# Windowed attention with two MLP layers on one core: the weight clamps of the first layer on GpSimd, and nine tiles' masks as a bf16 product

## The chip, the core and the metric

The kernel runs on one core of one Trainium2 chip. The metric is the device time of one execution in microseconds. TensorE is PE in the profile, VectorE DVE, ScalarE ACT, GpSimd POOL and SyncE SP; SP issues every load and store of this kernel.

## The reference, cut to what matters

Attention in a window of 32 keys to either side, with 32 global positions for each batch, then two MLP layers. B, H, Sl, Sg, D = 4, 8, 512, 32, 64.

```python
s_ll = scale * np.matmul(q_l, k_l.transpose(0, 1, 3, 2))
pos = np.arange(Sl)
mask = np.abs(pos[:, None] - pos[None, :]) <= window
s_ll = np.where(mask, s_ll, -1000000000.0)
s_lg = scale * np.matmul(q_l, k_g.transpose(0, 1, 3, 2))
a_l = sm(np.concatenate([s_lg, s_ll], axis=-1))
out_l = np.matmul(a_l, np.concatenate([v_g, v_l], axis=2))
...
h = x @ w_in                       # 512 -> 1024
solu = h * softmax(h)
ln = (solu - mu) / np.sqrt(var + 1e-06) * g_ln
x = ln @ w_out                     # 1024 -> 512
...
h = x @ w_in                       # 512 -> 2048
g = np.where(h >= 1, h, np.where(h <= -1, 0.0, (h + 1) ** 2 / 4))
out = g @ w_out                    # 2048 -> 512
```

All inputs are float32, the weights come as float64 words in pairs of 32-bit integers.

## The kernel before, in words

There are 16 tiles of 128 local positions and one more tile with the global positions of all four batches. The work goes through three stages that overlap.

**Attention**, tile by tile (`attention`, called with a tile and a part). `scores(t)` makes the scores of eight heads in a PSUM tile S (128 x 1024, two banks, from the ring psH of two, which the first MLP layer's h uses too): 32 small fp32 products, in which each block of 32 queries meets 128 keys. The outer blocks of 32 of these 128 keys need the window's triangles; the addition at L298 on VectorE puts them in. Then VectorE takes the maximum (nm), ScalarE the exponentials with their sum (e, rs). `gscores` makes the scores G of the global queries, `ptrans` transposes e (pPT), `pv` makes the output o and xn, `xtrans` transposes it into xy (pxT).

**The first MLP layer**, tile by tile in periods p: `b1` makes h with 24 products of 128x512 and the softmax and normalisation behind it, with a small power on GpSimd (rstd, L436) in the middle; `b3` transposes (plnT) and splits; `b4` makes yT for two tiles at a time. Products are made with split fp32r values: `split` writes a high part on ScalarE and the rest on GpSimd or VectorE (L137), and `mm3` adds three products.

**The second MLP layer** walks over 16 steps for each of three blocks of tiles (`h2`, `accum`), from 324 us on.

**Weights** come in pieces of 128x512. `fetch` issues a load of the double words into a staging buffer (raw), `convert` makes float32 of it: Abs on ScalarE (L147), a clamp of the exponent's range (L151), a shift (L155) and two combinations with the words (L157, L159), all four on VectorE, then for w_out of the first layer a scale on GpSimd (L163), then `split`. The first 16 pieces are those of the first MLP layer: eight of w_in in the lead, eight of w_out in the periods p = 0 to 3. The staging ring has three buffers, and SyncE's queue waits for L159, which frees one.

**What sets the order.** TensorE and SyncE run in the order in which the program is written, by small strings of letters: `START`, `LEAD_ORDER` for the first four tiles' attention (which also converts eight pieces), `ORDER_0` for p < 3 and `ORDER_1` behind. In period p, `attention` works on tile p + 4 and calls `scores(t + 2)`. On VectorE, ScalarE and GpSimd a scheduler orders the instructions; `behind` keeps a conversion behind an earlier VectorE instruction where `vec.gate` is set. `keep_warm` puts products of zeros (bf16, 128x512) ahead of the scores of the first five tiles.

The masks are built at the start on GpSimd, with 24 affine selects.

Of the kernel before, what the change touches and what calls it, by code (L numbers as in the profile page):

```python
# [8 lines left out]
F32 = mybir.dt.float32  # L9
# [51 lines left out]

STASH = range(5, 11)

WARM_S = [12, 4, 3, 4, 3]
WARM_P = [2, 5]

# [5 lines left out]
def kernel(ctx, tc, qk, vwin, qkg, vloc, vglo, w1i, w1o, g_ln, w2i, w2o, out):  # L72
# [13 lines left out]
    dram = ctx.enter_context(tc.tile_pool(name="dram", bufs=1, space=bass.MemoryType.DRAM))  # L86

    ident = const.tile([P, P], F32, name="ident")
    masks = const.tile([P, 3, 2, 32], F32, name="masks")
    nhalf = const.tile([P, 1], F32, name="nhalf")  # L90
    warm = const.tile([P, 1], F32, name="warm")
    gsb = const.tile([P, K1], F32, name="gsb")
# [10 lines left out]
    for c in range(4):  # L103
        for m in range(3):
            blk = masks[32 * c:32 * c + 32, m]
            nc.gpsimd.affine_select(out=blk[:, 0], in_=blk[:, 0], pattern=[[1, 32]], compare_op=ALU.is_ge, fill=NEG, base=0, channel_multiplier=-1)
            nc.gpsimd.affine_select(out=blk[:, 1], in_=blk[:, 1], pattern=[[-1, 32]], compare_op=ALU.is_ge, fill=NEG, base=0, channel_multiplier=1)
    nc.gpsimd.memset(masks[0:32, 1, 0], NEG)
    nc.gpsimd.memset(masks[96:128, 2, 1], NEG)

    class Ordered:

# [23 lines left out]
        act(out=hi, in_=src, func=AF.Copy)  # L136
        eng.tensor_tensor(out=lo, in0=src, in1=hi.bitcast(F32), op=ALU.subtract)  # L137

    def convert(weights, eng=nc.gpsimd):

        ws = []
        for (hi, lo), raw, scale in weights:
            t = stg.tile([P, 512], I32, tag="w32", name="w32")
            words = raw.rearrange("p (n two) -> p n two", two=2)
            ws.append((hi, lo, words[:, :, 0], words[:, :, 1], t, t.bitcast(F32), scale))
        for hi, lo, low, high, t, tf, scale in ws:
            first = nc.scalar.activation(out=tf, in_=high.bitcast(F32), func=AF.Abs)  # L147
            if vec.gate == "both" and vec.act is not None:
                behind(first, vec.act)
        for hi, lo, low, high, t, tf, scale in ws:  # L150
            first = nc.vector.tensor_scalar(tf, tf, WORD_LO, WORD_HI, ALU.max, ALU.min)  # L151
            if vec.gate and vec.last is not None:
                behind(first, vec.last)
        for hi, lo, low, high, t, tf, scale in ws:
            nc.vector.tensor_scalar(t, t, 3, 0x3FFFFFF8, ALU.logical_shift_left, ALU.bitwise_and)  # L155
        for hi, lo, low, high, t, tf, scale in ws:
            nc.vector.scalar_tensor_tensor(out=t, in0=high, scalar=-0x40000000, in1=t, op0=ALU.bitwise_and, op1=ALU.bitwise_or)  # L157
        for hi, lo, low, high, t, tf, scale in ws:
            nc.vector.scalar_tensor_tensor(out=t, in0=low, scalar=29, in1=t, op0=ALU.logical_shift_right, op1=ALU.bitwise_or)  # L159
        for hi, lo, low, high, t, tf, scale in ws:  # L160
            t3 = tf.rearrange("p (k n) -> p k n", k=hi.shape[1])
            if scale is not None:
                nc.gpsimd.tensor_tensor(out=t3, in0=t3, in1=scale.unsqueeze(2).to_broadcast(list(t3.shape)), op=ALU.mult)  # L163
            split(hi, lo, t3, eng)
# [11 lines left out]
            fetched.append((make, raw, scale))  # L176
        del todo[:n]

    def weights(n=1, eng=nc.gpsimd):
        while n > 0:  # L180
            m = min(n, 2)
            fetch(max(0, m - len(fetched)))
            convert([(make(), raw, scale) for make, raw, scale in fetched[:m]], eng)
            del fetched[:m]
            n -= m

# [94 lines left out]
    def scores(t):  # L281
        g = SEQ[t] % NB
        qT = qkT[t][:, :HP * P].rearrange("p (h c n) -> p h c n", h=HP, c=4)
        kT = key_blocks(t)
        S = psH.tile([P, 2, HP, P], F32, tag="H", name="S")
        if t < len(WARM_S):
            keep_warm(S[:, 0].rearrange("p h n -> p (h n)"), WARM_S[t])
        for hp in range(HP):
            for par in range(2):
                r = slice(64 * par, 64 * par + 64)  # L290
                for ci in range(4):
                    w = WSTART[ci]
                    mm(out=S[32 * ci:32 * ci + 32, par, hp], lhsT=qT[r, hp, ci],
                       rhs=kT[r, hp, w:w + 4].rearrange("p c d -> p (c d)"), start=True, stop=True)
        Sh = S.rearrange("p a h n -> p (a h) n")
        m = masks[:, 1 if g == 0 else 2 if g == NB - 1 else 0]
        edge = Sh.rearrange("p h (c d) -> p h c d", d=32)[:, :, 0:4:3]
        tt(out=edge, in0=edge, in1=m.unsqueeze(1).to_broadcast([P, H, 2, 32]), op=ALU.add)  # L298
        e = eT[t] = m1.tile([P, H, P], F32, tag="e", name="e", bufs=3)
        rs[t] = sm.tile([P, H], F32, tag="rs", name="rs")  # L300
        nm = sm.tile([P, H], F32, tag="nm", name="nm")
        vec.tensor_reduce(nm, Sh, AX.X, ALU.max, negate=True)
        vec.tensor_scalar(nm, nm, SCALE, None, ALU.mult)
        for h in range(H):
            act(out=e[:, h], in_=Sh[:, h], func=AF.Exp, bias=nm[:, h:h + 1], scale=SCALE, accum_out=rs[t][:, h:h + 1])
        vec.tensor_scalar(rs[t], rs[t], EPS_SM, None, ALU.add)
        vec.reciprocal(rs[t], rs[t])
# [276 lines left out]
    with tc.manual_schedule(engines={mybir.EngineType.PE, mybir.EngineType.SP}):  # L584
# [39 lines left out]
        for t in range(LEAD):  # L624
            n = CONV[t]
            for i, c in enumerate(LEAD_ORDER):
                if c in "012":
                    attention(t, int(c))
                elif c == "g":
                    attention(t, 4)  # L630
                elif c == "3" and t > 0:
                    attention(t - 1, 3)
                elif c == "w":
                    m = -(-n // LEAD_ORDER[i:].count("w"))
                    n -= m
                    weights(m)
                    fetch(3 + len(rooms) - len(fetched))


# [1 line left out]
        for p in range(NT):  # L641
# [3 lines left out]
            for i, c in enumerate(order):  # L645
# [18 lines left out]
                elif c == "4" and p >= 3:  # L664
                    b4(*divmod(p - 3, 2))
                elif c == "5" and p > 0:
                    b3(p - 1)
                elif c == "w":
                    if t == NL:
                        xtrans(NL)  # L670
                        at.close()
                        tc.swap_default_side()
                        w2ap = ExitStack()
                        w2a = w2ap.enter_context(tc.tile_pool(name="w2a", bufs=1, reuse_waits="tile"))
                        tc.swap_default_side()
                        weights2(15, in_pool(w2a))
                    m = -(-n // order[i:].count("w"))
                    n -= m
                    if todo or fetched:
                        weights(m)  # L680
                        fetch(3 + len(rooms) - len(fetched))
                    elif waiting or stashed or converted:
                        stash()
# [119 lines left out]
```

## Time and profile before

| | |
|---|---|
| runs | 718.05, 718.90 and 719.64 us, median 718.90 |
| the profiled execution | 718.96 us, its span 716.8 us |
| mean granted clock of TensorE | 0.983 |
| TensorE busy | 687.2 us, 96% of the span |
| weight loads of TensorE | 604.7 us, 84% |
| VectorE | 410.5 us, 57% |
| ScalarE | 311.3 us, 43% |
| GpSimd | 180.9 us, 25% |
| DMA | 72.54 MB, 101 GB/s over the span |

The span runs from the first to the last instruction; 2.2 us of the execution lie around it. A busy share is an average over stages with different limits, and is to be read by stretch.

### The profile page before, as it was taken

Reading aid. Unit: us, or ns where it says so; the run is one execution under the profiler, and the core shown is the slowest. Engines: PE = TensorE matmul, PEld = TensorE weight load, DVE = VectorE, ACT = ScalarE, POOL = GpSimd, SP = SyncE. Lnnn points to the kernel's source line nnn. Section 1 sums busy time; section 2 is a strip of 40 time slices with the busy share of each in tenths; the row PEclk is TensorE's granted clock in tenths of the full one; section 3 lists DMA queues with packets and bytes.
Section 4 is the critical chain, followed back from the end, with each engine's and each line's share of the span. In section 5 each row is a group of like instructions: output and inputs, shape, how many; then the busy total and the mean of one; then the engine's idle time right before and its main releaser. Section 6 shows DMA issues by size and latency. Waiting matters only on the chain.

```text
span 716.8 us, 15016 instructions
## 1 busy us (share of the span) xinstructions
PE 687.2 (96%) x6265; PEld 604.7 (84%) x6265; DVE 410.5 (57%) x735; ACT 311.3 (43%) x776; POOL 180.9 (25%) x197
## 2 busy tenths in 40 slices
PE   7788899999999999899999999999999999999997
PEld 4457688888888898889888889899999989999996
DVE  3987997577766559854977775432222234322232
ACT  5886664466646425433544433432222233222222
POOL 3233364111112213401222222222222222222210
PEclk8989999999999999999999999999999999999999
DMA  9788464444743073300422210020000001100002
GB/s 353 282 337 302 169 209 143 150 173 171 254 136 125 31 268 88 119 1 1 147 88 89 89 60 1 1 89 0 1 1 0 1 1 47 42 1 1 1 0 74
DMA packets 18932, 72.54 MB, mean 101 GB/s; under 512 B 2480, under 2 KB 3504, under 8 KB 16304
## 3 DMA queue, kind: packets, MB, share of 16 engines
q1 hardware_dynamic: 18864, 71.58, 28.2%
q8 instruction: 49, 0.80, 0.5%
q14 instruction: 19, 0.16, 0.1%
HBM read 63.71 MB, written 7.60 MB: 99 GB/s over the span
## 4 chain that ended last, share of the span: by engine, by line
PE 66%; DVE 15%; DMA 3%; issue 3%; ACT 2%; POOL 1%; SPq 0%; ACTq 0%; DVEq 0%; POOLq 0%
PE h L216 29%; PE acc L216 21%; PE yT L216 10%; DVE w L159 3%; DVE w L157 3%; DMA wraw<-in_w2o_dram 2%; DVE w L151 2%; PE plnT L447 2%; DVE xy L119 2%; DMA wraw<-in_w2i_dram 1%; PE o L348 1%; DVE e L119 1%; DVE w L155 1%; PE pPT L336 1%; DVE lnT L119 1%
## 5 line engine op out<-in xcount | busy, mean ns | idle before, releaser
L216 PE MATMUL h<-yT,w2i 128*128 128x384 f32 (+1 forms) x936 | 167.4, 327 | 1.6 <-DVE xy L119 1.6
L216 PEld LDWEIGHTS h<-yT,w2i 128*128 128x128 f32 x936 | 157.8, 188 | 9.1 <-DVE xy L119 3.1
L137 POOL TENSOR_TENSOR g<-xy,g 128x384 fp32r<-128x384 f32 (+1 forms) x92 | 91.9, 999 | 281.8 <-ACT g L128 253.3
L119 DVE TENSOR_SCALAR xy<-h 128x384 f32<-128x384 f32 (+1 forms) x96 | 51.1, 533 | 144.1 <-PE h L216 126.2
L216 PE MATMUL acc<-w2o,g 128*128 128x512 f32 x510 | 127.9, 394 | 0.0
L128 ACT ACTIVATE xy<-xy 128x384 f32<-128x384 f32 (+1 forms) x96 | 48.4, 504 | 145.0 <-DVE xy L119 144.8
L216 PEld LDWEIGHTS acc<-w2o,g 128*128 128x128 f32 x510 | 94.4, 188 | 17.2
L216 PE MATMUL h<-win,x 128*128 128x512 f32 x408 | 101.7, 404 | 1.8 <-issue 0.9
L216 PE MATMUL yT<-lnT,wout 128*128 128x256 f32 x768 | 95.7, 284 | 3.1 <-ACT xy L128 3.1
L216 PEld LDWEIGHTS yT<-lnT,wout 128*128 128x128 f32 x768 | 93.3, 191 | 4.0 <-ACT xy L128 3.6
L216 PEld LDWEIGHTS h<-win,x 128*128 128x128 f32 x408 | 76.4, 191 | 20.4 <-issue 1.1
L119 DVE TENSOR_TENSOR xy<-h,xy 128x384 f32<-128x384 f32 (+1 forms) x96 | 51.3, 534 | 56.4 <-ACT xy L128 56.4
L128 ACT ACTIVATE g<-xy 128x384 fp32r<-128x384 f32 (+1 forms) x96 | 48.7, 507 | 60.3 <-DVE xy L119 39.1
L128 ACT ACTIVATE e<-S,nm 128x128 f32<-128x128 f32 x128 | 45.1, 383 | 14.2 <-DVE nm L119 14.0
L147 ACT ACTIVATE w<-wraw 128x512 f32<-128x512 f32 x45 | 30.3, 681 | 30.5 <-DMA wraw<-in_w2o_dram 13.1
L137 POOL TENSOR_TENSOR x<-xy,x 128x512 fp32r<-128x512 f32 x17 | 22.5, 1325 | 70.2 <-ACT x L128 70.0
L216 PE MATMUL h<-yT,lnT 128*128 128x384 f32 (+1 forms) x216 | 38.8, 328 | 0.6 <-DVE xy L119 0.6
L216 PEld LDWEIGHTS h<-yT,lnT 128*128 128x128 f32 x216 | 36.5, 188 | 2.5 <-DVE xy L119 1.0
L216 PE MATMUL acc<-lnT,g 128*128 128x512 f32 x153 | 38.2, 393 | 0.0
L157 DVE SCALAR_TENSOR_TENSOR w<-wraw,w 128x512 int32<-128x512 int32 x45 | 36.1, 814 | 0.5
L159 DVE SCALAR_TENSOR_TENSOR w<-wraw,w 128x512 int32<-128x512 int32 x45 | 35.4, 789 | 0.4
L436 POOL TENSOR_TENSOR rstd<-rstd,nhalf 128x1 f32<-128x1 f32 x17 | 12.9, 759 | 85.7 <-DVE rstd L119 85.7
(115 smaller groups left out, 829.3 us busy)
## 6 DMA issues: line engine op xcount, KB each, us to landing
vw<-in_vwin_dram SPq DMA_DIRECT2D x16, 1024.0 KB, 5.8
qkT<-in_qk_dram SPq DMA_DIRECT2D x16, 832.0 KB, 7.9
wraw<-in_w2i_dram SPq DMA_DIRECT2D x16, 512.0 KB, 4.0
wraw<-in_w2o_dram SPq DMA_DIRECT2D x16, 512.0 KB, 3.6
wraw<-in_w1o_dram SPq DMA_DIRECT2D x8, 512.0 KB, 3.8
vn<-in_vloc_dram SPq DMA_DIRECT2D x4, 1024.0 KB, 8.3
out_dram<-o SPq DMA_DIRECT2D x16, 256.0 KB, 2.0
wraw<-in_w1i_dram SPq DMA_DIRECT2D x5, 512.0 KB, 9.7
```

Source lines behind the costliest of these rows:

```text
L119: self.last = getattr(nc.vector, name)(*args, **kw)
L128: vec.act = nc.scalar.activation(**kw)
L137: eng.tensor_tensor(out=lo, in0=src, in1=hi.bitcast(F32), op=ALU.subtract)
L147: first = nc.scalar.activation(out=tf, in_=high.bitcast(F32), func=AF.Abs)
L151: first = nc.vector.tensor_scalar(tf, tf, WORD_LO, WORD_HI, ALU.max, ALU.min)
L155: nc.vector.tensor_scalar(t, t, 3, 0x3FFFFFF8, ALU.logical_shift_left, ALU.bitwise_and)
L157: nc.vector.scalar_tensor_tensor(out=t, in0=high, scalar=-0x40000000, in1=t, op0=ALU.bitwise_and, op1=ALU.bitwise_or)
L159: nc.vector.scalar_tensor_tensor(out=t, in0=low, scalar=29, in1=t, op0=ALU.logical_shift_right, op1=ALU.bitwise_or)
L216: mm(out=dst, lhsT=pairs[i][0][x], rhs=pairs[i][1][y], start=start and j == 0, stop=stop and j == 3 * n - 1)
L336: nc.tensor.transpose(ps[:, hp], eT[t][:, HP * par + hp], ident)
L436: nc.gpsimd.tensor_tensor(rstd, rstd, nhalf, ALU.pow)
L447: nc.tensor.transpose(ps[:, k], ln[t][:, P * c:P * c + P], ident)
```

## The change

It moves the clamp of the first 16 weight pieces from VectorE to GpSimd, with the two bounds in the other order. And for tiles 1 to 9 it puts the mask into the scores on TensorE: the masks are now a bf16 tile of 128 keys' width (zero in the two middle blocks), and for each half of the heads one bf16 product of an identity with the mask opens the accumulation in PSUM, to which the scores are added. Tile 0 and tiles 10 to 15 keep the addition on VectorE. The mask's outer blocks are 0 and 3 instead of 0 and 1.

```diff
+MASK_PE = range(1, 10)
...
+    identb = const.tile([P, P], BF16, name="identb")
-    masks = const.tile([P, 3, 2, 32], F32, name="masks")
+    masks = const.tile([P, 3, 4, 32], BF16, name="masks")
...
+    nc.gpsimd.tensor_copy(identb, ident)
...
-    def convert(weights, eng=nc.gpsimd):
+    def convert(weights, eng=nc.gpsimd, clamp=nc.vector):
...
-            first = nc.vector.tensor_scalar(tf, tf, WORD_LO, WORD_HI, ALU.max, ALU.min)
-            if vec.gate and vec.last is not None:
+            first = clamp.tensor_scalar(tf, tf, WORD_HI, WORD_LO, ALU.min, ALU.max)
+            if clamp is nc.vector and vec.gate and vec.last is not None:
                 behind(first, vec.last)
         for hi, lo, low, high, t, tf, scale in ws:
-            nc.vector.tensor_scalar(t, t, 3, 0x3FFFFFF8, ALU.logical_shift_left, ALU.bitwise_and)
+            first = nc.vector.tensor_scalar(t, t, 3, 0x3FFFFFF8, ALU.logical_shift_left, ALU.bitwise_and)
+            if clamp is not nc.vector and vec.gate and vec.last is not None:
+                behind(first, vec.last)
...
+        kind = 1 if g == 0 else 2 if g == NB - 1 else 0
+        masked = t in MASK_PE
+        if masked:
+            m = masks[:, kind].rearrange("p c d -> p (c d)").unsqueeze(1).to_broadcast([P, HP, P])
+            for par in range(2):
+                mm(out=S[:, par], lhsT=identb, rhs=m, start=True, stop=False, skip_group_check=True)
...
-                       rhs=kT[r, hp, w:w + 4].rearrange("p c d -> p (c d)"), start=True, stop=True)
+                       rhs=kT[r, hp, w:w + 4].rearrange("p c d -> p (c d)"), start=not masked, stop=True, skip_group_check=masked)
...
-        m = masks[:, 1 if g == 0 else 2 if g == NB - 1 else 0]
-        edge = Sh.rearrange("p h (c d) -> p h c d", d=32)[:, :, 0:4:3]
-        tt(out=edge, in0=edge, in1=m.unsqueeze(1).to_broadcast([P, H, 2, 32]), op=ALU.add)
+        if not masked:
+            m = masks[:, kind, 0:4:3]
+            edge = Sh.rearrange("p h (c d) -> p h c d", d=32)[:, :, 0:4:3]
+            tt(out=edge, in0=edge, in1=m.unsqueeze(1).to_broadcast([P, H, 2, 32]), op=ALU.add)
...
-                    weights(m)
+                    weights(m, clamp=nc.gpsimd)
...
-                        weights(m)
+                        weights(m, clamp=nc.gpsimd if p < 4 else nc.vector)
```

The scheduler's order on VectorE moves too. Before, in the lead, around the maximum of tile 3's scores (S, nm; w32 is a piece in conversion, Sg and gnm belong to the global queries):

```order
L119 TENSOR_TENSOR S_521<-S_521,masks_82 128x8x2x32
L151 TENSOR_SCALAR w32_600<-w32_600 128x512
L119 TENSOR_REDUCE nm_561<-S_521 128x8
L155 TENSOR_SCALAR w32_600<-w32_600 128x512
L151 TENSOR_SCALAR w32_667<-w32_667 128x512
L119 TENSOR_SCALAR nm_561<-nm_561 128x8
L157 SCALAR_TENSOR_TENSOR w32_600<-wraw_379,w32_600 128x512
L119 TENSOR_REDUCE gnm_592<-Sg_187 128x2
```

The same place on VectorE with the change (L123 is the helper's line now, L159, L163 and L165 are the shift and the two combinations):

```order
L165 SCALAR_TENSOR_TENSOR w32_449<-xy2_91,w32_449 128x512
L123 RECIPROCAL rs_423<-rs_423 128x8
L159 TENSOR_SCALAR w32_515<-w32_515 128x512
L123 TENSOR_REDUCE nm_566<-S_525 128x8
L163 SCALAR_TENSOR_TENSOR w32_515<-xy1_90,w32_515 128x512
L123 TENSOR_SCALAR nm_566<-nm_566 128x8
L123 TENSOR_REDUCE gnm_597<-Sg_189 128x2
```

The addition and the clamps are gone, and the maximum of tile 3 stands before the conversions of pieces 4 and 5 (605 and 672), where it stood among them.

On GpSimd, at the first two periods' powers (rstd), before:

```order
L436 TENSOR_TENSOR rstd_1004<-rstd_1004,nhalf_83 128x1
L163 TENSOR_TENSOR w32_1127<-w32_1127,gsb_85 128x512
L137 TENSOR_TENSOR x_1630<-xy0_88,x_1630 128x512
L137 TENSOR_TENSOR wout1_186<-w32_1127,wout0_185 128x4x128
L436 TENSOR_TENSOR rstd_1179<-rstd_1179,nhalf_83 128x1
L163 TENSOR_TENSOR w32_1359<-w32_1359,gsb_85 128x512
```

And with the change (L155 is the clamp, L449 the power, L169 the scale, L141 the subtraction of `split`):

```order
L141 TENSOR_TENSOR x_1404<-xy0_89,x_1404 128x512
L449 TENSOR_TENSOR rstd_1011<-rstd_1011,nhalf_84 128x1
L169 TENSOR_TENSOR w32_1135<-w32_1135,gsb_86 128x512
L141 TENSOR_TENSOR wout1_188<-w32_1135,wout0_187 128x4x128
L141 TENSOR_TENSOR x_1640<-xy0_89,x_1640 128x512
L155 TENSOR_SCALAR w32_1595<-w32_1595 128x512
L449 TENSOR_TENSOR rstd_1187<-rstd_1187,nhalf_84 128x1
```

One clamp, that of piece 12 (1595), stands between the first period's work and the second period's power.

## Rows read from the trace of the kernel before

**Rows 1.** The page: engines over the span, and the chain that ended last.
```profile
PE 687.2 (96%) x6265; PEld 604.7 (84%) x6265; DVE 410.5 (57%) x735; ACT 311.3 (43%) x776; POOL 180.9 (25%) x197
...
PE 66%; DVE 15%; DMA 3%; issue 3%; ACT 2%; POOL 1%; SPq 0%; ACTq 0%; DVEq 0%; POOLq 0%
```

**Rows 2.** Busy time by stretch, cut where the tiles' h products begin.
```profile
core 0: us, PE busy (x) PEld busy (x) DVE busy (x) ACT busy (x) POOL busy (x), PEclk, DMA share, GB/s
20.00:59.63 39.63, 31.02 (x751) 22.40 (x739) 33.70 (x62) 32.98 (x112) 13.69 (x10) 0.91 0.82 308
59.63:74.26 14.63, 12.81 (x268) 10.13 (x269) 12.99 (x26) 7.80 (x27) 4.50 (x4) 1.00 0.69 251
74.26:90.16 15.90, 13.36 (x218) 10.90 (x216) 15.38 (x31) 12.56 (x37) 7.00 (x6) 0.92 0.57 196
90.16:109.23 19.07, 16.94 (x239) 15.21 (x237) 18.49 (x35) 11.07 (x33) 11.38 (x9) 0.95 0.63 217
109.23:126.23 17.00, 17.00 (x238) 15.17 (x237) 12.32 (x22) 9.06 (x30) 7.35 (x7) 0.93 0.33 117
```

**Rows 3.** The chain that ended last, 82 to 108 us: start, length, what.
```profile
103.91 0.80 DVE w L151
...
105.90 0.91 DVE w L151
...
107.87 0.33 PE plnT L447
```

**Rows 4.** VectorE's groups, 0 to 111 us: count, busy us, mean ns, idle before.
```profile
L151 DVE TENSOR_SCALAR w<-w 128x512 f32<-128x512 f32 x16 | 11.3, 714 | 1.5 <-ACT w L147 1.3
...
L119 DVE TENSOR_TENSOR S<-S,masks 128x512 f32<-128x512 f32 x10 | 6.9, 685 | 9.9 <-PE S L293 9.9
```

**Rows 5.** VectorE's timeline, single instructions: start, length, operation.
```profile
59.49 0.69 DVE L119 TENSOR_TENSOR S<-S,masks 128x512 f32<-128x512 f32 x1
60.09 1.28 DVE L119 BATCH_NORM_STATS2 st<-e 128x6 f32<-128x512 f32 x2
...
63.00 0.42 DVE L151 TENSOR_SCALAR w<-w 128x512 f32<-128x512 f32 x1
63.34 0.20 DVE L119 BATCH_NORM_AGGREGATE mv<-st 128x2 f32<-128x12 f32 x1
```

**Rows 6.** TensorE's timeline, merged: keep-warm products, and "o" twice.
```profile
21.73 1.03 PE L221 MATMUL S<-zero 128*128 128x512 bf16 x4
...
28.51 1.10 PE L348 MATMUL o<-vw,PT 128*32 128x64 f32 x64
...
39.58 1.93 PE L348 MATMUL o<-vw,PT 128*32 128x64 f32 x64
```

**Rows 7.** GpSimd's groups, 0 to 112 us, columns as in rows 4.
```profile
L137 POOL TENSOR_TENSOR win<-w,win 128x512 fp32r<-128x512 f32 x8 | 10.8, 1355 | 32.7 <-ACT win L128 32.7
L137 POOL TENSOR_TENSOR wout<-w,wout 128x512 fp32r<-128x512 f32 x7 | 10.2, 1461 | 3.1 <-ACT wout L128 3.1
L137 POOL TENSOR_TENSOR x<-xy,x 128x512 fp32r<-128x512 f32 x6 | 8.4, 1392 | 4.2 <-ACT x L128 4.1
L163 POOL TENSOR_TENSOR w<-w,gsb 128x512 f32<-128x512 f32 x7 | 7.6, 1082 | 5.3 <-DVE s L119 1.9 <-DVE w L159 1.8 <-issue 1.6
...
L107 POOL TENSOR_SCALAR_AFFINE_SELECT masks<-masks 32x32 f32<-32x32 f32 x12 | 2.5, 207 | 0.0
...
masks.py:199 POOL TENSOR_SCALAR_AFFINE_SELECT ident<-ident 128x128 f32<-128x128 f32 x1 | 0.3, 294 | 0.0
```

**Rows 8.** The timelines of VectorE and GpSimd at 28 us.
```profile
28.61 1.36 POOL L137 TENSOR_TENSOR x<-xy,x 128x512 fp32r<-128x512 f32 x1
...
28.76 1.50 DVE L151 TENSOR_SCALAR w<-w 128x512 f32<-128x512 f32 x1
```

**Rows 9.** The same: the masks' last instruction, and the first addition.
```profile
5.84 0.12 POOL L109 MEMSET masks<- 32x32 f32 x1
...
7.43 0.70 DVE L119 TENSOR_TENSOR S<-S,masks 128x512 f32<-128x512 f32 x1 [6.30 <-PE S L293]
```

More of the change, by code (lines that the diff above doesn't have):

```diff
@@ L106 @@
             nc.gpsimd.affine_select(out=blk[:, 0], in_=blk[:, 0], pattern=[[1, 32]], compare_op=ALU.is_ge, fill=NEG, base=0, channel_multiplier=-1)
-            nc.gpsimd.affine_select(out=blk[:, 1], in_=blk[:, 1], pattern=[[-1, 32]], compare_op=ALU.is_ge, fill=NEG, base=0, channel_multiplier=1)
+            nc.gpsimd.affine_select(out=blk[:, 3], in_=blk[:, 3], pattern=[[-1, 32]], compare_op=ALU.is_ge, fill=NEG, base=0, channel_multiplier=1)
     nc.gpsimd.memset(masks[0:32, 1, 0], NEG)
-    nc.gpsimd.memset(masks[96:128, 2, 1], NEG)
+    nc.gpsimd.memset(masks[96:128, 2, 3], NEG)
+    nc.gpsimd.tensor_copy(identb, ident)
     class Ordered:
@@ L177, in fetch, with weights @@
         del todo[:n]
-    def weights(n=1, eng=nc.gpsimd):
+    def weights(n=1, eng=nc.gpsimd, clamp=nc.vector):
         while n > 0:
@@ L182, in weights @@
             fetch(max(0, m - len(fetched)))
-            convert([(make(), raw, scale) for make, raw, scale in fetched[:m]], eng)
+            convert([(make(), raw, scale) for make, raw, scale in fetched[:m]], eng, clamp)
             del fetched[:m]
```

## The prediction

> **What bounds the kernel now.** I read the page first. TensorE is busy for 96% of the span, VectorE for 57%; the chain that ended last lies on TensorE for 66% and on VectorE for 15% [rows 1]. An average like this hides stages, so the next view is the busy time by stretch [rows 2]. I cut it where the first-layer products of a tile (h, 24 matmuls) begin: the lead without its first 20 us, then the periods that I call p1, p2 and p3, then one more. The reader is to see two things there. From 109.23 us on TensorE is busy all the time (17.00 of 17.00 us), so VectorE's work is hidden there, and only TensorE's own work counts. Between 20 and 109.23 us TensorE stands idle for 8.61 + 1.82 + 2.54 + 2.13 = 15.1 us, and VectorE is nearly full: 33.70 of 39.63, 12.99 of 14.63, 15.38 of 15.90, 18.49 of 19.07 us. The chain there runs through VectorE's queue, instruction after instruction, the clamps among them, until TensorE's plnT at 107.87 us takes it over [rows 3]. So this kernel gets faster by what leaves VectorE before 109 us, as far as TensorE, ScalarE and GpSimd let it. All work behind starts from there and moves with it, since nothing later depends on absolute time.
>
> **What leaves VectorE.** All 16 clamps and ten mask additions lie before 111 us [rows 4]; the change takes 16 clamps and nine of the additions (tiles 1 to 9; the first stays). Durations overlap in the queue, so the price is from one start to the next: a clamp 63.34 - 63.00 = 0.34 us, an addition 60.09 - 59.49 = 0.60 us [rows 5]. By stage, counting starts:
> - Before 20 us: one clamp and two additions. VectorE waits for scores and loads there, and I take nothing.
> - Lead: seven clamps, three additions: 2.4 + 1.8 = 4.2 us. ScalarE is busy for 32.98 of 39.63 us there and the DMA share is 0.82 [rows 2], so they bind soon. I take half, 2.1 us; the ends are 0 and 4.2.
> - p1: one clamp, two additions: 1.5 us. p2: two clamps, one addition: 1.3 us. p3: five clamps: 1.7 us. The ninth addition starts behind 109 us, where TensorE binds: nothing.
>
> **What TensorE gets.** Two bf16 products of 128x512 for each of nine tiles, with a load of the identity each. The keep-warm products have the same shape and type: four take 1.03 us, so 0.26 us each and 0.52 us a tile [rows 6]. Two tiles (1 and 2) fall before 20 us beside other waits; seven fall between 20 and 109 us, 3.6 us in all: four in the lead and one each in p1, p2, p3. There they set a floor: TensorE's busy time plus 0.52 us. p1: 12.81 + 0.52 = 13.3, against 14.63: room 1.3. p2: 13.9 against 15.90: room 2.0. p3: 17.5 against 19.07: room 1.6. So the periods give 1.3 + 1.3 + 1.6 = 4.2 us. In the lead the floor is 31.02 + 2.1 = 33.1 us of 39.63, and the 2.1 us fit. The scores now add to what stands in the bank; their number and shape stay, so that costs nothing.
>
> **What GpSimd gets.** No row shows this clamp on GpSimd. The nearest by kind is its affine select, with one input: 0.207 us for 32 columns, 0.294 us for 128 [rows 7], so 0.9 ns a column and 0.64 us for 512. The ends are 0.29 us (the 128 columns as they are) and 1.36 us (the mean of two-input win). I take 0.64, since the clamp has one input. The Trainium skill (GPSIMD Engine Reference, section 3.1) gives 1.03 cycles an element for short bodies, an estimate of 0.44 us at its 1.2 GHz; the sum would hardly move. Fifteen clamps after 20 us are 9.6 us of GpSimd, whose busy time in the stages to 109 us is 13.69 + 4.50 + 7.00 + 11.38 = 36.6 of 89 us [rows 2]: it has room.
>
> The price is what this does to VectorE. A clamp on VectorE that meets a GpSimd subtraction stretches: at 28.76 us it took 1.50 us, until 0.29 us after the subtraction that ran from 28.61 to 29.97 us [rows 8]. The 16 clamps took 11.3 us; at the 0.42 us of one that ran alone they would have taken 6.7, so 4.6 us are such stops [rows 4, 5], against 10.8 + 10.2 + 8.4 + 7.6 = 37.0 us of big GpSimd work [rows 7]: 0.12 us a microsecond. VectorE's other instructions are stopped as well, so I take twice that, 0.25: the new clamps then cost VectorE 9.6 x 0.25 = 2.4 us. Against it stand the 4.6 us: a removed clamp no longer stops, but the next instruction may; behind it is often a reduce that reads PSUM, so I count half, 2.3 us. The two cancel, and I set them at nothing together; the ends are 4.6 us gained and 9.6 us lost.
>
> The clamp also puts a wait in: VectorE's shift (L159 in the new numbering) now waits for GpSimd, where the clamp waited for ScalarE. Queued behind the shift are the reduces of S and h, for which ScalarE waits. And a clamp now stands in GpSimd's queue ahead of the second tile's "rstd", for which VectorE waits already. The clamp needs only ScalarE's Abs, which runs early, so I price this at nothing; one clamp late behind a subtraction would cost about 1.4 us. The building of the masks gets a cast and a longer memset, some 0.4 us by the rows for 128 columns; it ended at 5.96 us and the first addition starts at 7.43 [rows 9]. Loads on SyncE's queue that wait for a staging buffer are freed by the same conversions, earlier if anything.
>
> **The sum.** 2.1 + 4.2 + 0 = 6.3 us off the profiled execution of 718.96 us (span 716.8 and 2.2 around it): 712.7. The median of the runs is 718.9, the same within 0.1 us, so 712.6.
>
> **Rivals.**
> - TensorE fills up altogether: with shorter waits the whole 15.1 us of idle time go, less 3.6 us of products: 11.5 us, 707.4. For it: the stages show little else than VectorE in the way, and part of TensorE's busy time is slow clock: the 64 "o" products took 1.10 us at 28.51 and 1.93 at 39.58 us, behind idle time [rows 6], in a stretch whose mean granted clock is 0.91, between 1.2 and 2.4 GHz. Less idle time could give that back. Against: ScalarE's load in the lead. Chance 0.20.
> - No change that counts (within 0.2%, 1.4 us; about what a measurement of this kernel can tell): the waits are of latency, through PSUM buffers and ScalarE, VectorE's relief is half of what I count, 3.2 us, and the 3.6 us of products lie on the path: 719.3. For it: VectorE itself idles 1.6 us in p1. Against: the chain of [rows 3] has no gap on VectorE worth the name. Chance 0.15.
> - Slower: each clamp on GpSimd stops VectorE for its whole length, because VectorE is full and nearly always in the middle of a conversion that reads SBUF. It decides from 6.3 / 15 = 0.42 us of stop per clamp on. At 0.64 us it is 9.6 - 6.3 = 3.3 us slower, 722.2; at 1.36 us, 14.1 us slower, 733. For it: the 1.50 us row. Against: the average of 0.25, since many of VectorE's instructions there read PSUM. Chance 0.13. The Trainium skill (SBUF — State Buffer, section "SBUF: two separate sides") has this rule: VectorE and GpSimd share a pair of SBUF ports as an exclusive lock, held for the whole instruction, and the loser fully blocks, where VectorE's instruction is of a two-port mode or has two SBUF inputs. By that rule the case is this one; the row at 28.76 us agrees, as it ends just behind GpSimd's.
>
> **How the numbers follow.** My forecast has 0.52; its own range is 709.5 to 717 (the lead's 0 to 4.2 us, and the stops by some 2 us either way). Faster by over 0.2% (below 717.5) are it and the first rival: 0.72. Same 0.15, slower 0.13. The range for 8 in 10 reaches to the first rival's time, 707.4, and into the second's, to 719.5; it leaves out the slower case, and times below the first rival's.
>
> **What would show it.** Right: TensorE's idle time between 20 us and the start of its full stretch falls from 15 to about 6 us; the full stretch begins with the fifth h product (109.23 us now) near 103 us; the clamps on GpSimd last 0.5 to 0.8 us; VectorE's busy time before that point falls by some 10 us; 18 new products of 0.26 us. Wrong: VectorE's conversions stretch as GpSimd's clamps run, or its shifts wait for GpSimd; or the periods keep their length with VectorE idle in them, which would mean that ScalarE or PSUM buffers bound them; or time comes back behind 109 us, where I expect none to move.

## The result: slower by 0.9%

The changed kernel took 724.89 us, median of four runs (724.00 to 725.69), beside 718.47 us (717.71 to 719.64) of the kernel before: ratio 1.009, 95% interval [1.0074, 1.0106]. The forecast was 712.6 us, the range 707.4 to 719.5. The profiled execution has a span of 723.5 us, 6.7 more than before, and a mean granted clock of 0.981. The page of after, where [rows 1] show before:

```profile
PE 690.1 (95%) x6283; PEld 606.1 (84%) x6283; DVE 404.2 (56%) x710; ACT 312.5 (43%) x776; POOL 191.0 (26%) x214
...
PE 67%; DVE 15%; DMA 7%; ACT 5%; issue 4%; POOL 1%; SPq 0%; ACTq 0%; DVEq 0%; POOLq 0%
```

VectorE lost 25 instructions, GpSimd got 17 and TensorE 18, as the change says. In the chain DMA rose from 3 to 7% and ScalarE from 2 to 5%: a hint that something waits for a load. Busy time by stretch, after, cut at the same h products and with the columns of [rows 2]:

```profile
20.00:67.05 47.05, 33.92 (x696) 24.93 (x696) 31.07 (x49) 33.61 (x112) 20.57 (x20) 0.82 0.75 286
67.05:83.43 16.38, 13.02 (x271) 10.12 (x271) 13.47 (x25) 8.52 (x28) 5.12 (x5) 1.00 0.44 159
83.43:99.40 15.97, 14.07 (x219) 11.24 (x218) 14.24 (x29) 11.87 (x36) 8.63 (x9) 0.89 0.55 191
99.40:116.06 16.66, 16.55 (x242) 14.49 (x240) 16.08 (x27) 10.99 (x32) 12.12 (x11) 1.00 0.59 207
116.06:133.55 17.49, 16.00 (x239) 14.35 (x238) 12.77 (x22) 9.53 (x30) 6.33 (x6) 1.00 0.51 194
```

Against [rows 2] the lead is longer by 47.05 - 39.63 = 7.42 us, p1 by 1.75 and p2 by 0.07; p3 is shorter by 2.41. That is 6.83 us, by which the fifth h product starts later (116.06 against 109.23), and the span's end is 6.7 later: nothing of it is made or lost behind. VectorE is busy for less of the lead now (31.07 us, 33.70 before), yet the lead is longer. So the loss is to be looked for in the lead, and not in VectorE's own work.

**Where the lead lost it.** TensorE's timeline around the first h products, before:

```profile
45.01 0.45 PE L323 MATMUL G<-qkT,qkg 64*32 64x128 f32 x16
46.15 1.10 PE L348 MATMUL o<-vw,PT 128*32 128x64 f32 x64 [0.69 <-ACT xy L128]
47.18 1.66 PE L216 MATMUL h<-win,x 128*128 128x512 f32 x6
```

and after:

```profile
47.78 0.45 PE L336 MATMUL G<-qkT,qkg 64*32 64x128 f32 x16
53.77 1.93 PE L361 MATMUL o<-vw,PT 128*32 128x64 f32 x64 [5.54 <-ACT xy L132]
55.63 6.87 PE L222 MATMUL h<-win,x 128*128 128x512 f32 x24
```

TensorE waits 5.54 us, where it waited 0.69, for ScalarE's copy xy. Behind the wait "o" takes 1.93 us instead of 1.10; the mean granted clock between 40 and 60 us is 0.64, where it was 0.92 (1.0 is 2.4 GHz, 0.5 is 1.2). ScalarE's timeline says why. Before:

```profile
44.83 0.79 ACT L128 ACTIVATE win<-w 128x512 fp32r<-128x512 f32 x1
45.35 0.75 ACT L128 ACTIVATE xy<-pxT 128x512 f32<-128x512 f32 x1
45.82 0.61 ACT L128 ACTIVATE Sg<-G 128x128 f32<-128x128 f32 x2
...
51.60 0.66 ACT L128 ACTIVATE win<-w 128x512 fp32r<-128x512 f32 x1
52.12 1.24 ACT L147 ACTIVATE w<-wraw 128x512 f32<-128x512 f32 x2
```

After:

```profile
44.42 0.59 ACT L132 ACTIVATE PT<-pPT 128x512 f32<-128x512 f32 x1
45.42 0.63 ACT L132 ACTIVATE win<-w 128x512 fp32r<-128x512 f32 x1 [0.41 <-DVE w L165]
48.78 0.63 ACT L132 ACTIVATE win<-w 128x512 fp32r<-128x512 f32 x1 [2.73 <-DVE w L165]
52.58 0.66 ACT L151 ACTIVATE w<-wraw 128x512 f32<-128x512 f32 x1 [3.16 <-DMA wraw<-in_w1o_dram]
53.14 0.58 ACT L132 ACTIVATE xy<-pxT 128x512 f32<-128x512 f32 x1
```

The last win and the Abs of the first w_out piece (L151, wraw) stood behind xy and behind tile 5's eight exponentials; the scheduler now has put both ahead of xy. The last win waits 2.73 us for VectorE's combination (L165), the Abs then 3.16 us for its load, and xy, for which TensorE waits, stands behind both. The chain of after runs through that load:

```profile
42.08 10.42 DMA wraw<-in_w1o_dram
...
52.58 0.66 ACT w L151
53.23 0.49 ACT xy L132
...
53.77 1.93 PE o L361 x64
```

**The periods.** TensorE's waits in p1 (the first two) and p2 (the third), before:

```profile
69.84 0.65 PE L394 MATMUL og<-vn,PgT 128*32 128x64 f32 x32 [1.13 <-ACT Sg L128]
...
73.85 0.66 PE L447 MATMUL plnT<-ident,e 128*128 128x128 f32 x4 [0.43 <-DVE ogn L119]
...
85.66 0.23 PE L325 MATMUL G<-qkg 64*32 64x32 f32 x4 [2.20 <-ACT PgT L128]
```

and after:

```profile
77.62 0.65 PE L407 MATMUL og<-vn,PgT 128*32 128x64 f32 x32 [1.51 <-ACT Sg L132]
...
83.02 0.66 PE L460 MATMUL plnT<-ident,e 128*128 128x128 f32 x4 [1.23 <-DVE ogn L123]
...
94.96 0.23 PE L338 MATMUL G<-qkg 64*32 64x32 f32 x4 [1.90 <-ACT PgT L132]
```

All three waits were there before. In p1 TensorE's idle time rose from 1.82 to 3.36 us: the two waits are longer by 0.38 and 0.80 us, and an idle stretch of 0.61 us that the trace puts down to nothing comes in at 79.95 us. What made the two waits longer is not shown. In p2 idle time fell from 2.54 to 1.90 us, the wait for ScalarE's PgT, but busy time rose from 13.36 to 14.07 us (the mean granted clock was 0.89, 0.92 before), so p2 kept its length.

**What the moved work costs.** Groups of VectorE and of GpSimd, after, 0 to 125 us (columns as in [rows 4]), and one mask's products on TensorE:

```profile
L163 DVE SCALAR_TENSOR_TENSOR w<-wraw,w 128x512 int32<-128x512 int32 x13 | 12.3, 949 | 0.1
...
L165 DVE SCALAR_TENSOR_TENSOR w<-wraw,w 128x512 int32<-128x512 int32 x13 | 11.8, 910 | 0.2
L159 DVE TENSOR_SCALAR w<-w 128x512 int32<-128x512 int32 x16 | 10.1, 634 | 1.7 <-POOL w L155 1.7
```

```profile
L155 POOL TENSOR_SCALAR w<-w 128x512 f32<-128x512 f32 x16 | 10.8, 684 | 17.6 <-ACT w L151 17.6
```

```profile
73.62 0.59 PE L299 MATMUL S<-masks,identb 128*128 128x512 bf16 x2
74.15 1.16 PE L305 MATMUL S<-qkT 64*32 64x128 f32 x64
```

A clamp on GpSimd takes 0.68 us in the mean, 0.60 when nothing disturbs it (the row at 36.68 us below); a mask's two products take 0.59 us, and 0.53 from their start to that of the scores. VectorE's three other conversion instructions of the 16 pieces got longer: with the three pieces whose first words lie in xy (2.6 + 2.2 us), 39.0 us, where the same groups before sum to 31.5 us. So 7.5 of the 11.3 us that the clamps took of VectorE [rows 4] came back as longer neighbours. Fourteen of these instructions took over 0.1 us longer than one alone (0.42 us a shift, 0.69 us a combination). Thirteen of them end 0.28 us (shifts) or 0.55 us (combinations) behind a subtraction or a scale that GpSimd did before the change too; only one, the combination at 38.86 us, ends behind a clamp. One stop by a subtraction, first on GpSimd, then on VectorE:

```profile
36.68 0.60 POOL L155 TENSOR_SCALAR w<-w 128x512 f32<-128x512 f32 x1
37.26 1.28 POOL L141 TENSOR_TENSOR win<-w,win 128x512 fp32r<-128x512 f32 x1
```

```profile
37.32 1.51 DVE L159 TENSOR_SCALAR w<-w 128x512 int32<-128x512 int32 x1
```

The shift starts 0.06 us behind GpSimd's subtraction and ends 0.29 us behind it, as the clamp of [rows 8] did; the next shift, at 42.55 us, takes 0.42 us. It is the next instruction that is stopped, as the clamp was. The clamps themselves stop little: that one combination by 0.33 us and three small scalings (rs at 23.93 us, nm at 27.60 and 37.02) by 0.41, 0.42 and 0.14 us, against 0.17 and 0.15 us alone; an estimate of 1.3 us from these rows. And they are stopped in turn: the longest, 1.05 us at 44.81 us, ends 0.47 us behind a combination of VectorE.

### The profile page after: what moved, and what is told of

Same layout as the page of the kernel before. It is cut to its first block, busy times and chain, and to the rows that moved or that the text cites. A ratio compares the mean times of both kernels' runs of the same rounds, so it can differ in the third digit from the quotient of the medians.

```text
span 723.5 us, 15043 instructions
## 1 busy us (share of the span) xinstructions
PE 690.1 (95%) x6283; PEld 606.1 (84%) x6283; DVE 404.2 (56%) x710; ACT 312.5 (43%) x776; POOL 191.0 (26%) x214
## 4 chain that ended last, share of the span: by engine, by line
PE 67%; DVE 15%; DMA 7%; ACT 5%; issue 4%; POOL 1%; SPq 0%; ACTq 0%; DVEq 0%; POOLq 0%
PE h L222 29%; PE acc L222 20%; PE yT L222 9%; DVE w L163 3%; DVE w L165 3%; DMA wraw<-in_w2i_dram 2%; DMA wraw<-in_w2o_dram 2%; ACT e L132 2%; PE o L361 2%; PE plnT L460 2%; DVE e L123 2%; DMA wraw<-in_w1o_dram 1%; DVE xy L123 1%; ACT w L151 1%; DVE w L155 1%
## 5 line engine op out<-in xcount | busy, mean ns | idle before, releaser
L141 POOL TENSOR_TENSOR g<-xy,g 128x384 fp32r<-128x384 f32 (+1 forms) x92 | 92.2, 1002 | 281.2 <-ACT g L132 261.8
L123 DVE TENSOR_SCALAR xy<-h 128x384 f32<-128x384 f32 (+1 forms) x96 | 51.1, 533 | 144.4 <-PE h L222 126.5
L123 DVE TENSOR_TENSOR xy<-h,xy 128x384 f32<-128x384 f32 (+1 forms) x96 | 51.3, 534 | 56.4 <-ACT xy L132 56.4
L151 ACT ACTIVATE w<-wraw 128x512 f32<-128x512 f32 x45 | 30.0, 677 | 30.8 <-DMA wraw<-in_w2i_dram 13.2
L141 POOL TENSOR_TENSOR x<-xy,x 128x512 fp32r<-128x512 f32 x17 | 22.3, 1313 | 72.0 <-ACT x L132 71.9
L163 DVE SCALAR_TENSOR_TENSOR w<-wraw,w 128x512 int32<-128x512 int32 x45 | 39.0, 875 | 0.5
L165 DVE SCALAR_TENSOR_TENSOR w<-wraw,w 128x512 int32<-128x512 int32 x45 | 37.4, 833 | 0.5
L449 POOL TENSOR_TENSOR rstd<-rstd,nhalf 128x1 f32<-128x1 f32 x17 | 12.0, 707 | 81.6 <-DVE rstd L123 73.3
```

Of the source, the lines that this page charges most:

```text
L123: self.last = getattr(nc.vector, name)(*args, **kw)
L449: nc.gpsimd.tensor_tensor(rstd, rstd, nhalf, ALU.pow)
```

## The experiments

Theory: the scheduler's new order on ScalarE, with load-bound instructions ahead of xy, costs what is lost. Rivals: the stops of VectorE by GpSimd's clamps (the slower rival of the prediction), and the masks' products on TensorE. Each kernel was timed beside the kernel before on the same chip; that one's medians in the four groups of runs are 717.5, 716.9, 716.6 and 718.5 us. Of a ratio the interval tells whether it is clear of 1.

### The two halves, each alone

The first edit leaves the clamps of the change alone, the other two leave its masks alone.

```diff
-MASK_PE = range(1, 10)
+MASK_PE = range(0)
...
-                    weights(m, clamp=nc.gpsimd)
+                    weights(m)
...
-                        weights(m, clamp=nc.gpsimd if p < 4 else nc.vector)
+                        weights(m)
```

> The change with the clamps on GpSimd alone; all masks stay additions on VectorE. In ScalarE's queue the Abs of the first w_out piece still stands ahead of tile 5's exponentials, but now behind the copy of tile 2's transpose (xy). Theory A (the loss is ScalarE's order: that Abs waits 3.2 us for its load, and the copy and the exponentials wait behind it): most of the 5.54 us hole of TensorE ahead of tile 3's output is gone, part of the loss stays; 719 to 721.5 us. Rival B (the loss is GpSimd stopping VectorE): the loss stays whole, 724 to 727 us, with VectorE's conversions stretched. Rival C (the loss is TensorE's mask products): no loss is left, 714 to 718 us.

> The change with the mask products alone; all clamps stay on VectorE. In ScalarE's queue the Abs of the first w_out piece stands behind tile 5's exponentials again. Theory A: no hole behind the loads, VectorE is relieved by nine additions of 0.60 us, 715 to 718.5 us. Rival B: no loss either, 715 to 718.5 us. Rival C (18 products of 0.26 us and their loads lie on the path): 722 to 726 us.

Clamps alone: 716.10 us, ratio 0.9984 [0.9964, 1.0005]. Masks alone: 719.13 us, 1.0027 [1.0007, 1.0047]. Neither loses what both lose: -0.16% and +0.27% stand beside +0.9%. So neither the clamps nor the products lose this much by themselves. But each half gets an order of its own from the scheduler too (in neither is xy behind the Abs; the wait ahead of "o" is below 0.4 us in both), so these runs don't price the halves cleanly. Both expectations missed: the clamps alone came in below the 719 to 721.5 us of theory A, in the range given to the rival of the products, and the masks alone between theory A's range (to 718.5) and that rival's (from 722).

### The change, with one or two instructions held back

The Abs of the first period's w_out pieces is kept behind the last exponential of tile 5 (e3); then also the high part of the last w_in piece (e4).

```diff
+            if vec.hold is not None:
+                behind(first, vec.hold)
...
+            vec.hold = lead_exp if p == 0 else None
...
+                    vec.after = vec.exp if t == LEAD - 1 and i > LEAD_ORDER.index("1") else None
```

> The whole change, with one order pinned: the Abs of the first w_out pieces stands behind tile 5's last exponential in ScalarE's queue; VectorE's and TensorE's orders stay those of the change. Theory A: the copy of tile 2's transpose starts at 49.4 instead of 53.14 us, tile 3's output and the h products follow, 3.5 to 4 us come back: 720.5 to 721.5 us. Rivals B and C: 724 to 725.5 us, as the order of one Abs is not what costs.

> The run before, with a second order pinned: the high part of the lead's last w_in piece stands behind tile 5's exponentials too, so that the copy of tile 2's transpose waits for neither the load nor that piece's conversion. Theory A: the copy starts at about 46.2 us, tile 3's output at 48 us as before the change; the first h product then ends where its last weights let it, near 57 us instead of 62.4: 5 to 6 us back, 718.5 to 720 us. Rivals B and C: 724 to 725.5 us.

With the Abs held: 721.39 us, 1.0052 [1.0033, 1.0070]; TensorE's wait ahead of "o" falls from 5.54 to 3.49 us. With both: 720.70 us, 1.0032 [1.0013, 1.0051]; that wait is 0.31 us, and h starts at 50.35 us instead of 55.63. Two constraints on ScalarE's order, no work taken away, give back some 0.6 of the 0.9% (by the medians 3.2 of 6.4 us are left). The second constraint's own share is not clear of noise, as the two intervals overlap; 720.70 us also lies above the 718.5 to 720 expected, so something else of the loss was left.

### The kernel before, with that one instruction moved

ScalarE's order is written down as a chain of constraints, the kernel before's own but for the Abs of the first w_out piece, which stands ahead of xy (on VectorE xn moved by two places in consequence).

```diff
+        for i, j in zip(ACT_ORDER, ACT_ORDER[1:]):
+            behind(acts[j], acts[i])
```

> The kernel before, nothing of the change in it; in ScalarE's queue one instruction is moved, the Abs of the first w_out piece ahead of the copy of tile 2's transpose, where the change has it. Theory A: the copy starts near 52.5 instead of 45.35 us, tile 3's output near 53 instead of 46.15, the second h product at 64 to 66 instead of 59.63 us: 722 to 725 us. Rivals B and D: the place of one Abs costs nothing much, 717 to 719.5 us.

722.68 us, ratio 1.0080 [1.0061, 1.0100]: with no clamp and no mask moved, nearly the whole loss of the change (1.009). TensorE's timeline of this kernel, at the place shown above:

```profile
44.80 0.45 PE L337 MATMUL G<-qkT,qkg 64*32 64x128 f32 x16
51.70 1.93 PE L362 MATMUL o<-vw,PT 128*32 128x64 f32 x64 [6.45 <-ACT xy L140]
53.56 7.62 PE L230 MATMUL h<-win,x 128*128 128x512 f32 x24
```

The same signature: a wait of 6.45 us for xy, then "o" in 1.93 us.

### The change and its halves, in the orders of before

Now both ScalarE's and VectorE's orders of the lead and the first periods are held to those of before, the removed instructions left out. TensorE and SyncE go by the program anyway; GpSimd's order is left to the scheduler, and differs from that of after in a few places.

```diff
+        for i, j in zip(ACT_ORDER, ACT_ORDER[1:]):
+            behind(acts[j], acts[i])
+        kept = [vec.all[i] for i in DVE_ORDER if vec.all[i] is not None]
+        for i, j in zip(kept, kept[1:]):
+            behind(j, i)
```

> The whole change, with ScalarE's and VectorE's instructions pinned in the order that they had before the change (those that the change takes away left out). Theory A (the loss is the order that the scheduler made of ScalarE's queue in the lead and in p2): the hole ahead of tile 3's output and the long p2 are gone, 715 to 718 us, at or under the kernel before. Rival B (GpSimd stops VectorE; it showed 7.8 us more on shifts and combinations in the change): the stops stay, 719 to 722 us. Rival D (an order that suits the old kernel does not suit the new one, since the clamps' results come later): VectorE waits for GpSimd's clamps by more than 3 us in sum, 719 us or more.

> The mask products alone, ScalarE's and VectorE's orders pinned to those before. Theory A: the masks alone, without a new order, relieve VectorE by 0.60 us nine times: 714.5 to 717.5 us. Rival C (the products cost on TensorE what they save on VectorE): 717.5 to 719.5 us.

> The clamps on GpSimd alone, ScalarE's and VectorE's orders pinned to those before. Theory A: 714 to 717 us, as the clamps leave VectorE. Rival B: VectorE's other conversions stretch by as much as the clamps took, and the shift waits for GpSimd: 717 to 720 us.

The change: 715.40 us, 0.9980 [0.9959, 1.0002]. Masks alone: 717.49 us, 1.0007 [0.9990, 1.0024]. Clamps alone: 714.41 us, 0.9963 [0.9944, 0.9982], the one that beats both kernels. The same work as in after, in the old orders, is 1.1% faster than after (0.998 beside 1.009, some 8 us): the order is the cause of the loss, shown from both sides. The move of one Abs by itself gives 0.8%; the change with two constraints (1.0032) is still slower than with both orders held (0.9980), and where that rest lies is not shown. By the ratios the work itself is worth 2.6 us for the clamps, nothing measurable for the masks (717.49 us stands between the two expectations and does not decide between them), and 1.4 us for both, not clear of no change.

### What the relief is worth without its price

Clamps of the 16 pieces left out altogether (e10), masks of tiles 1 to 9 left out altogether (e11), both in the orders of before.

```diff
+            if clamp is None:
+                vec.all.append(None)
+                continue
...
-            for par in range(2):
-                mm(out=S[:, par], lhsT=identb, rhs=m, start=True, stop=False, skip_group_check=True)
```

> The kernel before with the clamps of the first 16 weight pieces left out altogether, on VectorE and on GpSimd (that part of the computation is missing), the masks added on VectorE, and the orders of ScalarE and VectorE those of before. It shows what VectorE's relief is worth when GpSimd is not given the clamps. Clamps alone with the same orders took 714.4 us beside a before of 716.9 (ratio 0.996). Theory, the clamps on GpSimd stop VectorE and so give back most of the relief: about 15 clamps of 0.61 us stretch the other three conversions by some 7 us in sum, of which about half lies on the path, so this run is 3 to 4 us below that one, near 711 (ratio 0.992). Rival, the stops are hidden and the relief itself is worth little because ScalarE, loads and PUSH-down to TensorE bind the periods: within 1 us of that run, 713.5 to 715 (ratio 0.995 to 0.9975). Busy time of shift and both combinations of the 16 pieces on VectorE: 31 to 33 us by the first (before 31.3, clamps alone 37).

> The kernel before with the masks of tiles 1 to 9 left out altogether, neither addition nor product (that part of the computation is missing), the clamps on VectorE, and the orders of ScalarE and VectorE those of before. It shows what the additions cost. Masks by the product with the same orders came out like before (ratio 1.0007). Theory, the products take back what the additions' absence gives: nine additions of 0.6 us less, of which some 2 to 4 us lie on the path, and the product pairs of 0.59 us are 5.3 us of TensorE: ratio 0.995 to 0.997, some 713.5 to 715 beside a before of 717. Rival, the additions were hidden and their absence is worth nothing, and the products are hidden too: ratio 0.999 to 1.001, the same time as with the products.

No clamps: 713.33 us, 0.9950 [0.9937, 0.9962]; no masks: 715.12 us, 0.9972 [0.9960, 0.9984]. VectorE's groups of the 13 pieces with words of their own and the shifts, with clamps on GpSimd in the old orders (shift, then the combinations):

```profile
L188 DVE TENSOR_SCALAR w<-w 128x512 int32<-128x512 int32 x16 | 11.4, 717 | 0.6 <-POOL w L183 0.6
L193 DVE SCALAR_TENSOR_TENSOR w<-wraw,w 128x512 int32<-128x512 int32 x13 | 10.8, 841 | 0.1
L195 DVE SCALAR_TENSOR_TENSOR w<-wraw,w 128x512 int32<-128x512 int32 x13 | 9.3, 719 | 0.1
```

and without any clamp:

```profile
L196 DVE SCALAR_TENSOR_TENSOR w<-wraw,w 128x512 int32<-128x512 int32 x13 | 10.8, 836 | 0.1
L191 DVE TENSOR_SCALAR w<-w 128x512 int32<-128x512 int32 x16 | 10.0, 633 | 0.8 <-ACT w L178 0.8
L198 DVE SCALAR_TENSOR_TENSOR w<-wraw,w 128x512 int32<-128x512 int32 x13 | 9.6, 742 | 0.1
```

With the three other pieces the sums are 35.8 and 34.6 us, beside 31.5 before. So the theory of the first expectation falls: of the 4.3 us by which the neighbours grew, 3.1 are there with no clamp on any engine. These are the stops by GpSimd's old subtractions and scales, which hit the shift, and in part the combinations, when the clamp is gone. One of them in the kernel without clamps, GpSimd's subtraction and VectorE's shift:

```profile
34.74 1.27 POOL L168 TENSOR_TENSOR win<-w,win 128x512 fp32r<-128x512 f32 x1 [2.21 <-ACT win L158]
```

```profile
35.27 1.02 DVE L191 TENSOR_SCALAR w<-w 128x512 int32<-128x512 int32 x1
```

All eight of its conversion instructions that took over 0.1 us longer than alone end 0.28 us (shifts) or 0.55 us (combinations) behind such a one. With clamps on GpSimd the sum is 1.2 us larger, but there too no conversion with over 0.1 us of stop ends behind a clamp; the shift meets a subtraction five times instead of four. The times are 1.1 us apart (714.41 and 713.33, with intervals that overlap). The relief itself is worth only 3.3 us. For the masks the absence of additions is worth 2.0 us (0.28% of 717), and with the products in their place nothing is left: the two intervals, [0.9960, 0.9984] and [0.9990, 1.0024], don't touch.

### Why the products cost anything

In all these profiles TensorE has idle stretches in the middle of a run of like products that the trace puts down to nothing ("issue"). The one ahead of, or within, the first h products, in the kernel before and in the change with the old orders:

```profile
49.74 2.26 PE L216 MATMUL h<-win,x 128*128 128x512 f32 x9 [0.90 <-issue]
```

```profile
48.56 0.43 PE L393 MATMUL o<-vw,PT 128*32 128x64 f32 x4 [2.29 <-issue]
```

Without masks' products it stands after 6 of 24 h; with them before the last 4 of 64 "o", ten products earlier, and ten products of masks were issued by then. So two kernels shift the count by products of zeros at the start, where TensorE waits for its first load: the kernel before with ten more (e12), and the masks in the old orders with 66 more (e13).

```diff
-            keep_warm(S[:, 0].rearrange("p h n -> p (h n)"), WARM_S[t])
+            if t == 0:
+                keep_warm(S[:, 0].rearrange("p h n -> p (h n)"), 10)
+                for _ in range(12):
+                    mm(out=S[:, 0].rearrange("p h n -> p (h n)")[:, :64], lhsT=zero[:, :P], rhs=zero[:, :64], start=True, stop=True)
```

> The kernel before with ten products more in TensorE's order: the first twelve keep-warm products become ten, and twelve small ones of 128x64 bf16 zeros follow them, while TensorE waits for its first load; on ScalarE two entries at the very start change places, the other engines keep their orders. In every run without the masks' products TensorE has idle stretches that the profile puts down to nothing (issue), at the same three places of its order: after 2 of 8 pPT products at 21 us, after 6 of 24 of the first h products, after 12 of 64 o products at 70 us; in runs with the masks' products they stand 4, 10 and 13 products earlier, which is the number of mask products issued by then plus none or one. Theory, the place is fixed by the count of instructions that TensorE has got from the start: here all three places come 10 products earlier, so the second stands before the last 4 of the 64 o products ahead of the first h, and none is left within h; the time is within 0.3% of before (ratio 0.998 to 1.003), as the stretch moves and does not vanish. Rival, the place depends on data or on the work around it: the second stretch stays after 6 of 24 h products.

> The masks by products alone, clamps on VectorE, ScalarE and VectorE in the order of before, and 66 products more in TensorE's order at the start: the first twelve keep-warm products become four, and 74 small ones of 32x32 bf16 zeros follow. Without the 66 this kernel took 717.5 us beside a before of 716.9 (ratio 1.0007), and its profile had an idle stretch of 2.13 us without a cause shown before the last 4 of the 64 o products, ahead of the first h; with neither additions nor products the ratio was 0.9972. Theory, the products cost nothing of their own, they only bring such stretches to places where TensorE would not wait otherwise: here the stretch falls among the G products, just ahead of a wait for xy of some 1.15 us, so a part of it is hidden; ratio 0.997 to 0.999, with h of the lead starting near 48 us instead of 50.2. Rival, the masks' products themselves take TensorE's time: ratio 0.9995 to 1.002 as without the 66, wherever the stretch stands. If the lead's start is late by the small products themselves (first scores after 7 us instead of 6.1), as much is added to either.

Ten more: 722.02 us (718.87 to 725.36), ratio 1.0050 [1.0030, 1.0071]. 66 more: 717.71 us, 0.9992 [0.9975, 1.0009]. TensorE's rows of the kernel with ten more:

```profile
21.71 0.32 PE L353 MATMUL o<-vw,PT 128*32 128x64 f32 x8 [3.34 <-issue]
...
49.25 0.30 PE L353 MATMUL o<-vw,PT 128*32 128x64 f32 x4 [1.45 <-issue]
...
72.59 1.09 PE L353 MATMUL o<-vw,PT 128*32 128x64 f32 x62 [0.20 <-issue]
```

All three stand ten products earlier than in kernels without masks' products. The kernel before's own profile shows only the one in h; for the others the profile of the clamps alone in the old orders serves (after 2 of 8 pPT at 21.04 us, which became before the last 8 "o"; after 12 of 64 "o" at 69.81 us, which became after 2). In every profile that has a stretch at one of these places, TensorE has as many weight loads behind it there (351 to 352, 862 to 863, 1243 to 1245), with and without masks and zeros. So the place of these three goes by the count of TensorE's instructions: the theory's first half is shown. Another, after 4 of 8 pPT near 11.8 us, kept its place in the program (0.46 us before, 1.28 with ten more) and is not of this kind. The second half missed: I had expected no change in time, and the kernel with ten products of zeros, beside a wait, is 0.5% slower, some 3.6 us. On ScalarE two early instructions changed places as well, so that price is not the products' alone for certain. With 66 more the stretch ahead of h is gone (h starts at 47.16 us, 50.17 without), but others stand earlier (2.88 us at 12.36, 2.89 at 19.49), and the ratio can't be told from that without them (1.0007).

What stays open: how much of the masks' 2.4 us (717.49 - 715.12, each beside a before of about 717) is TensorE's time for 18 products, and how much such stretches in worse places. Their lengths differ from kernel to kernel between 0.2 and 3.3 us, and the one profiled execution of a kernel need not be a typical one (that of the ten more, 718.87 us, is the fastest of its twelve; that of the change in the old orders, 720.80 us, the slowest).

## Why the prediction was wrong

- **The step that failed** is the one on the clamp's wait: "The clamp needs only ScalarE's Abs, which runs early, so I price this at nothing". I had looked at how the orders of VectorE and GpSimd moved, and took ScalarE's as it was. There the scheduler moved the Abs of the first w_out piece ahead of xy, where it waits 3.16 us for its load, and TensorE 5.54 us for xy. That one move costs 0.8% by itself, put into the kernel before; the new orders together cost 1.1%, some 8 us of the 12.3 us between forecast and measurement. The rest is relief that was sized too high: with the old orders held the change gives 1.4 us where the sum had 6.3.
- **What leaves VectorE** was counted rightly (25 instructions), but its worth too high. Without any price the clamps' absence gives 3.3 us and the additions' 2.0, 5.3 together if they add up, against 2.1 + 4.2 = 6.3 us.
- **The stops.** I set them off at nothing: 2.4 us more by the new clamps, 2.3 us of 4.6 given back by the old ones. The new clamps stop VectorE for some 1.3 us in after (the estimate above), and of the 4.6 us 3.1 went to the neighbours, where I had half. In the old orders VectorE's neighbours are 1.2 us longer with the clamps on GpSimd, so the two sides still nearly cancel (1.5 gained, 1.2 lost). In after they did not: the neighbours were 7.5 us longer, by 13 stops of old subtractions and scales and one of a clamp. The Trainium skill (SBUF — State Buffer, section "SBUF: two separate sides") has the loser of the ports stopped for the whole of the other's instruction; the shift at 37.32 us, 1.51 us long and done 0.29 us behind the subtraction, agrees.
- **The clamp on GpSimd**, 0.64 us, measured 0.60 alone and 0.68 in the mean; **a mask's products**, 0.52 us, measured 0.59. Both ends of the clamp's range (0.29 and 1.36) were far off. The products were to fit into the periods' room and cost nothing; in the old orders they took back the additions' whole 2.0 us.
- **The periods.** p3 came to 16.66 us, below the floor of 17.5 (the granted clock was 1.00 there, 0.95 before). p1 (13.3 forecast, 16.38) and p2 (13.9, 15.97) missed. The sum let TensorE's idle time in them vanish with VectorE's work; in p1 its waits grew, and in p2 a wait of 1.90 us for ScalarE's PgT was left. TensorE's idle time from 20 us to the fifth h product was to fall from 15 to 6 us; it rose to 13.13 + 3.36 + 1.90 + 0.11 = 18.5 us.
- **Behind 109 us nothing moves**: right in sum, 6.83 us late there and 6.7 at the end. But TensorE is not full from the fifth h product on: at 132.70 us it waits 1.49 us for VectorE's xn. Before, such a wait, of 2.13 us, stood in p3; without it p3 is shorter.
- **The slower rival** (GpSimd's lock, from 722.2 us) gives about the measured time by a mechanism that does not decide it: in the old orders the kernel with those clamps on GpSimd is 0.37% faster than before, and taking them away altogether gives 1.1 us more.

## What to carry to other kernels

Where a scheduler orders an engine's instructions, compare the orders of all engines after an edit, those it does not touch first, and look for an instruction that waits for a load and now stands ahead of a copy for which TensorE waits. Price an edit with the old orders held, so that the edit and the new order are told apart: here they were -0.2% and +1.1%. Relief of an engine that is stopped by another is worth less than its busy time, since the next instruction is stopped instead: with 11.3 us of clamps taken off VectorE, 3.1 us came back with nothing put in their place.

## What the runs showed of the hardware that was not expected

TensorE stops at fixed places of its instruction count: three such idle stretches, with nothing that the trace shows to wait for, stand ten products earlier when ten are put in at the start, and the kernel with those ten, which lie beside a wait, is 0.5% slower. The traces also hold the transfers of the DMA queue that the profile calls "instruction", 49 of 16 KB in after. In all profiles each stretch at one of the three places ends 1.2 to 1.6 us behind the landing of such a transfer, always the second, the sixth and the ninth. Between the first two places, four transfers apart, lie some 510 weight loads and as many products, 255 instructions to a transfer, 64 bytes for one. So the stretches look like waits for TensorE's instructions; that the transfers cause them is not shown, as no run moves a transfer by itself.
